# Weight fetches tied to the softmax in a fused attention and network kernel, with the first unit's normalisation on another engine

## The chip, the cores and the metric

The kernel runs on one core of a Trainium2 chip. A core has a matrix engine (TensorE, PE in the profile, with its weight loads as PEld), a vector engine (VectorE, DVE), a scalar engine (ScalarE, ACT), a general engine (GpSimd, POOL) and a queue that issues transfers (SyncE, SP). The first four work from SBUF, the on-chip memory; matmuls write to PSUM, which is handed out in banks. The metric is the device time of one execution in microseconds.

## The reference

Attention over 4 batches, 8 heads, 768 positions and 64 columns a head, in which each query sees the first four keys (the sinks) and a window of 128 keys that ends at itself; then a two-layer network on the 3072 tokens, 512 to 2048 to 512. All is float32.

```python
scores = scale * np.matmul(q, k.transpose(0, 1, 3, 2))
keep = is_sink | in_window
scores = np.where(keep, scores, -1000000000.0)
a = np.exp(scores - np.max(scores, axis=-1, keepdims=True))
a = a / (np.sum(a, axis=-1, keepdims=True) + 1e-09)
x = np.matmul(a, v)            # then heads side by side: 3072 x 512
h = x @ w_in
out = np.maximum(0.01 * h, h) @ w_out
```

The weights come as float64, that is as pairs of 32-bit words, and the kernel turns them into float32 itself.

## The kernel before

**Units.** The 3072 tokens are cut into eight units of 384 (half a batch each), and a unit has three blocks of 128 queries (T = 3). Attention runs unit by unit and head by head. The network runs one unit behind: while it works on unit u, attention works on unit u + 1. So there is a first stretch with attention alone.

**Attention, units 0 and 1 (`attend_early`).** For each block: scores on TensorE (L266), masked reduction on DVE which finds the row's maximum (L278; it becomes `anchor[0]`), exponential with row sum on ACT (L280). After three blocks `normalise_early` makes the reciprocals on DVE (L283, L284) and multiplies the probabilities: in unit 0 on DVE (L290), in unit 1 on ACT (L288). The tail transposes the probabilities on TensorE (L338, L339, L342), ACT copies them out of PSUM (L340, L343), POOL gathers the sinks' columns (L346), and `values` multiplies with the values (L407, L411). Tails and values of a head are put on a list and taken from it between the scores of the next head, so that TensorE has work while a softmax runs. In unit 0 the scores use four PSUM banks by turns, later one.

**Attention, units 2 to 7 (`attend_late`).** Here each operand is split into a rounded high part (fp32r) and the rest, and the parts are multiplied separately: `split_head` (L231 on ACT, L232 and L234 on POOL) for queries and keys, `split_values` (L245 on ACT, L246 on POOL) for the values of a pair of heads, at the even head of the pair. The tails are L351, L358 on ACT, L359 on DVE and L320 on POOL.

**Network (`mlp_stream`).** Sixteen slices `fc` of 128 hidden columns: matmuls into `h` (L525), leaky ReLU on ACT and DVE (L532, L533), split into `gh` and `gl` (L534, L535), matmuls into `o` (L546). A slice has seven steps, 112 a unit (`mlp_steps`); an attention unit has 60 (`att_steps`), and the attention's steps are dealt out between those of the network. The network starts after 70 steps of attention (60 + LEAD0).

**Weights.** There are 32 tiles of 512 KB of words, `wi` and `wo` of each slice. `load_weights(fc)` fetches both tiles of a slice on SP (L152, L153), decodes each with three DVE instructions (L169, L171, L173; the word is put together in PSUM bank `d`), rounds on ACT (L177) and subtracts on POOL (L178). A fetch waits until the decode four tiles back is done (DEPTH); the first four have no such wait. Slices 0 and 1 are asked for in the first stretch, the others by the network's first unit, two slices ahead. `check_weights` fetches all 32 tiles again in units 2 to 5, to see whether they lie in the range that the decoder handles (L187 on ACT, L189 on POOL, L191 on DVE).

**Order of work.** TensorE's instructions run in the order written. Those of the other engines are ordered when the program is built, by a planner with a model of costs and due times; each engine and SP's queue then take them strictly in that order. `tc.issue_after(anchor[0].ins)` keeps a decode behind the latest reduction on DVE. A dependency added by `tc.add_manual_dep` is a real wait on the chip.

**Banks for transpositions.** `slot()` hands them out: in the first stretch (phase 0) `t` and `h` by turns, then (phase 1) only `t`, and once every weight tile has been asked for (phase 2) `t` and the decoder's `d` by turns.

Of the kernel before, what the change touches and what calls it, by code (L numbers as in the profile page):

```python
# [9 lines left out]
F32 = mybir.dt.float32  # L10
F32R = mybir.dt.float32r
I32 = mybir.dt.int32
I8 = mybir.dt.int8
AF = mybir.ActivationFunctionType
ALU = mybir.AluOpType
# [5 lines left out]
P = 128  # L21
# [5 lines left out]
NFC = DF // P  # L27
# [27 lines left out]
PRE = 2  # L55
WARM = 22
DEPTH = 4
PRE0 = 24
PRED = 12
W_LO = 1.125 * 2.0 ** -15  # L60
W_HI = 1.875 * 2.0 ** 16
# [51 lines left out]
def fast_path(ctx, tc, cpool, qk, vu, vs, w_in, w_out, out, ident, wz, lim, masks, tri, diag, negm, wmin, wmax):  # L113
    nc = tc.nc
    wpool = ctx.enter_context(tc.tile_pool(name="wpool", bufs=1))
# [3 lines left out]
    iopool = ctx.enter_context(tc.tile_pool(name="iopool", bufs=2))  # L119
# [3 lines left out]
    ps_t = ctx.enter_context(tc.tile_pool(name="ps_t", bufs=1, space=PSUM))  # L123
# [22 lines left out]
    wts = {}  # L146
    anchor = [None]

    def fetch(raw, nm, fc):
        if nm == "i":  # L150
            src = w_in.rearrange("(c p) f -> p c f", p=P)[:, :, 2 * fc * P:2 * (fc + 1) * P]
            return nc.sync.dma_start(out=raw.rearrange("p (c f) t -> p c (f t)", c=NCC), in_=src)  # L152
        return nc.sync.dma_start(out=raw.rearrange("p f t -> p (f t)"), in_=w_out[fc * P:(fc + 1) * P, :])  # L153

    decoded = []

    def load_weights(fc):
        for nm in ("i", "o"):
            raw = wpool.tile([P, 512, 2], I32, tag=f"w{nm}{fc}", name=f"w{nm}raw{fc}")
            dma = fetch(raw, nm, fc)  # L160
            if len(decoded) >= DEPTH:
                tc.add_manual_dep(dma.ins, decoded[-DEPTH].ins.name,
                                  mybir.DependencyInfo(mybir.DependencyClass.Sync, mybir.DependencyReason.SCHED_ONLY),
                                  reason="pace")
            top, low = raw[:, :, 1], raw[:, :, 0]
            word = ps_t.tile([P, 512], I32, tag="d", name=f"d{nm}{fc}")
            w = iopool.tile([P, 512], F32, tag="io", name=f"w{nm}f{fc}")
            with tc.issue_after(anchor[0].ins):
                nc.vector.tensor_scalar(out=word, in0=top, scalar1=3, scalar2=0x3FFFFFFF,  # L169
                                        op0=ALU.logical_shift_left, op1=ALU.bitwise_and)  # L170
            nc.vector.scalar_tensor_tensor(out=word, in0=top, scalar=-0x40000000, in1=word,  # L171
                                           op0=ALU.bitwise_and, op1=ALU.bitwise_or)
            decoded.append(nc.vector.scalar_tensor_tensor(out=w.bitcast(I32), in0=low, scalar=29, in1=word,  # L173
                                                          op0=ALU.logical_shift_right, op1=ALU.bitwise_or))
            both = wpool.tile([P, 2, 512], F32R, tag=f"w{nm}{fc}", name=f"w{nm}{fc}")
            hi, lo = both[:, 0, :], both[:, 1, :]
            nc.scalar.copy(out=hi, in_=w)  # L177
            nc.gpsimd.tensor_tensor(out=lo, in0=w, in1=hi.bitcast(F32), op=ALU.subtract)  # L178
            wts[nm, fc] = (hi, lo)

    def check_weights(nm, fc):
        raw = iopool.tile([P, 512, 2], I32, tag="wraw", name=f"c{nm}raw{fc}", bufs=1)
        fetch(raw, nm, fc)
        mag = iopool.tile([P, 512], F32, tag="io", name=f"mag{nm}{fc}")
        zero = iopool.tile([P, 512], F32, tag="io", name=f"zero{nm}{fc}")
        col = (NFC if nm == "o" else 0) + fc
        nc.scalar.activation(out=mag, in_=raw.bitcast(F32)[:, :, 1], func=AF.Abs,  # L187
                             accum_out=wmax[:, col:col + 1])
        nc.gpsimd.tensor_scalar(out=zero, in0=mag, scalar1=0.0, scalar2=None, op0=ALU.is_equal)  # L189
        with tc.issue_after(anchor[0].ins):  # L190
            nc.vector.tensor_tensor_reduce(out=zero, in0=mag, in1=zero, scale=1.0, scalar=3.0e38,  # L191
                                           op0=ALU.add, op1=ALU.min, accum_out=wmin[:, col:col + 1])
# [45 lines left out]
    def split_values(u, h):  # L238
        vr, sr = vraws.pop((u, h))
        vsp = apool.tile([P, 4, 2 * P], F32R, tag="vsp", name=f"vsp{u}_{h}", bufs=1)  # L240
        ssp = apool.tile([SKR, 1, 2 * P], F32R, tag="ssp", name=f"ssp{u}_{h}", bufs=1)
        for dst, src, m in ((vsp, vr, NVB[u % 2]), (ssp, sr, 1)):
            sview = src[:, 0:m * P].rearrange("p (n q c) -> p n q c", q=2, c=D)
            hview = dst.rearrange("p n (q c) -> p n q c", c=D)[:, 0:m, 0::3, :]
            nc.scalar.copy(out=hview, in_=sview)  # L245
            nc.gpsimd.tensor_tensor(out=dst[:, 0:m, D:3 * D].rearrange("p n (q c) -> p n q c", c=D),  # L246
                                    in0=sview, in1=hview.bitcast(F32), op=ALU.subtract)
        return vsp, ssp
# [33 lines left out]
    def normalise_early(u, w, sm):  # L282
        nc.vector.tensor_scalar(out=sm, in0=sm, scalar1=1e-9, scalar2=None, op0=ALU.add)  # L283
        nc.vector.reciprocal(out=sm, in_=sm)  # L284
        for j in range(T):
            p = w[:, j, :] if u % 2 or j else w[:, j, WM:]
            if u:
                nc.scalar.mul(p, p, sm[:, j:j + 1])  # L288
            else:
                nc.vector.tensor_scalar(out=p, in0=p, scalar1=sm[:, j:j + 1], scalar2=None, op0=ALU.mult)  # L290

    def softmax(u, h, j, ps, w):
        if KSL[u % 2][j][1] == W3:
# [151 lines left out]
    def attend_late(u, h, pend, state):  # L445
        odd = h % 2
        sp = split_head(u, h)
        state = state[h // 2 % 2]
        if not odd:
            state["v"] = split_values(u, h)  # L450
            state["sk"] = apool.tile([P, T, 2, NSK], F32, tag="sk", name=f"sk{u}_{h // 2}")
        load_next(u, h)
        pk = apool.tile([P, T, WM], F32, tag="pk", name=f"pk{u}_{h}", bufs=PKB)
        sk = state["sk"]
        pt = apool.tile([P, 2, 2 * TU], F32R, tag="pt", name=f"pt{u}_{h}")
        state["pt", odd] = pt
        for j in range(T):
            ps = scores(u, h, j, (0, TU + NK[u % 2]), sp)
            softmax(u, h, j, ps, pk[:, j, :])
            yield  # L460
            at = len(pend) - (VSW and j == 0 and not odd and len(pend) > 0)
            pend.insert(at, (0, lambda j=j: tail(u, h, j, pk, pt, sk)))
# [46 lines left out]
    def mlp_stream():  # L509
        po = {}  # L510
        prev = None
        for step in range(NU * NFC + 1):
            u, fc = divmod(step, NFC)
            cur = None
            if u < NU:
                if u == 0:
                    while len(wts) < 2 * min(NFC, fc + 1 + AHEAD):
                        load_weights(len(wts) // 2)
                wh, wl = wts["i", fc]
                ph = ps_h.tile([P, 512], F32, tag="h", name=f"h{u}_{fc}")  # L520
                for cc in range(NCC):
                    xh, xl = xs[u][cc]
                    cs = slice(cc * P, (cc + 1) * P)
                    for c, (w, x) in enumerate(((wh, xh), (wh, xl), (wl, xh))):
                        nc.tensor.matmul(ph[:, 0:TU], lhsT=w[:, cs], rhs=x, start=cc == 0 and c == 0,  # L525
                                         stop=cc == NCC - 1 and c == 2)
                    if cc < NCC - 1:
                        yield
                g = mpool.tile([P, TU], F32, tag="g", name=f"g{u}_{fc}")
                gh = mpool.tile([P, TU], F32R, tag="gh", name=f"gh{u}_{fc}", bufs=2)  # L530
                gl = mpool.tile([P, TU], F32R, tag="gl", name=f"gl{u}_{fc}", bufs=2)
                nc.scalar.mul(g, ph[:, 0:TU], 0.01)  # L532
                anchor[0] = nc.vector.tensor_tensor(out=g, in0=ph[:, 0:TU], in1=g, op=ALU.max)  # L533
                nc.scalar.copy(out=gh, in_=g)  # L534
                (nc.gpsimd if u == 0 else nc.vector).tensor_tensor(out=gl, in0=g, in1=gh.bitcast(F32), op=ALU.subtract)  # L535
                cur = (u, fc, gh, gl)
                yield
# [35 lines left out]
    done = 0  # L573
    while done < att_steps + LEAD0:
        done += 1
        next(stream)
        if done >= PRE0 and len(wts) < 2 * min(PRE, (done - PRE0 + 1) // PRED):
            load_weights(len(wts) // 2)
    phase[0] = 1
    for x, _ in enumerate(mlp_stream()):  # L580
        if len(wts) == 2 * NFC:
            phase[0] = 2
        due = att_steps + LEAD0 + att_steps * (x + 1) // mlp_steps
        due += min(LEAD - LEAD0, (LEAD - LEAD0) * (x + 1) // mlp_steps)
        while done < due:
            done += 1
            next(stream, None)
# [200 lines left out]
```

## Time and profile before

| what | value |
|---|---|
| median of the runs | 740.24 us (738.78 to 741.04, 3 runs) |
| the profiled execution | 740.5 us |
| its span, first to last instruction | 738.6 us, 12473 instructions |
| PE busy | 712.1 us, 96% |
| PEld busy | 622.7 us, 84% |
| DVE busy | 547.8 us, 74% |
| ACT busy | 422.6 us, 57% |
| POOL busy | 371.2 us, 50% |
| moved by DMA | 77.77 MB, mean 105 GB/s |
| mean granted TensorE clock | 0.988 |

The profile is one execution. Each row of a timeline gives the start and duration in us, the engine, the line of the kernel (L290), the operation, output and input tiles with their shapes, how many instructions were joined (x3), and in brackets how long the engine stood before and for whom. The view of waits gives us in total, the number of times and the longest. The view of stretches gives busy time of each engine between two moments, then the granted TensorE clock (1.00 is full speed), the share of the DMA engines and GB/s. The chain of waits is followed back from the last instruction. Idle time of an engine that nobody waits for costs nothing.

### The profile page before, as it was taken

To read this page: it belongs to the slowest core of one execution; us is meant where nothing else is said; L and a number is where in the kernel's file an instruction comes from. 1 tells how busy PE (TensorE), PEld (TensorE's weight loads), DVE (VectorE), ACT (ScalarE), POOL (GpSimd) and SP (SyncE) were. 2 spreads that over 40 slices of the span, in tenths; PEclk is the share of its full clock that TensorE was granted. 3 is DMA by queue.
4 is the path that set the end of the run, shared out by engine and by line. 5 is a ranking of instruction groups with operands and counts; after the bars stand their busy time and mean duration, and the time that the engine had idled before them with its cause. 6 is when DMAs were issued, how large, how long until landed. Compare 5 with 4: busy or idle time off the path is not lost.

```text
span 738.6 us, 12473 instructions
## 1 busy us (share of the span) xinstructions
PE 712.1 (96%) x3871; PEld 622.7 (84%) x3871; DVE 547.8 (74%) x1749; ACT 422.6 (57%) x1178; POOL 371.2 (50%) x500
## 2 busy tenths in 40 slices
PE   6889999899999999999999999999999999999996
PEld 4547887689999988999988988999988999989995
DVE  6678888656667898888888988888888978733222
ACT  4566666657665566656666566666666565522221
POOL 2025556745555676756657676756566556300000
PEclk9899999999999999999999999999999999999999
DMA  8466667122112333324343343324332221001001
GB/s 295 120 208 199 211 207 231 57 87 73 50 55 69 128 108 110 115 87 157 95 126 109 114 126 123 101 100 138 115 111 94 88 69 41 0 1 43 1 1 48
DMA packets 43755, 77.77 MB, mean 105 GB/s; under 512 B 3616, under 2 KB 26400, under 8 KB 43680
## 3 DMA queue, kind: packets, MB, share of 16 engines
q1 hardware_dynamic: 43536, 76.76, 32.8%
q8 instruction: 33, 0.54, 0.3%
q14 instruction: 42, 0.34, 0.1%
q10 hardware_dynamic: 144, 0.13, 0.1%
HBM read 70.58 MB, written 6.29 MB: 104 GB/s over the span
## 4 chain that ended last, share of the span: by engine, by line
PE 82%; DVE 9%; DMA 3%; ACT 3%; issue 1%; SPq 0%; POOL 0%; ACTq 0%; DVEq 0%
PE h L525 32%; PE o L546 32%; PE v L407 8%; PE s L266 6%; PE t L351 2%; DVE gl L535 2%; DMA qkn<-in_qk 1%; DVE zeroi L191 1%; PE v L411 1%; DVE g L533 1%; DMA vsraw<-in_vs 1%; PE t L338 1%; DVE pe L278 0%; DVE xf L419 0%; DVE pk L311 0%
## 5 line engine op out<-in xcount | busy, mean ns | idle before, releaser
L525 PE MATMUL h<-xh,wi 128*128 128x384 f32 x1024 | 314.5, 354 | 1.5 <-DVE g L533 1.5
L546 PE MATMUL o<-wo,gh 128*128 128x512 f32 x768 | 244.9, 400 | 0.0
L525 PEld LDWEIGHTS h<-xh,wi 128*128 128x128 f32 x1024 | 190.5, 188 | 14.4 <-DVE g L533 2.6
L525 PE MATMUL h<-xl,wi 128*128 128x384 f32 x512 | 172.7, 337 | 0.0
L546 PE MATMUL o<-wo,gl 128*128 128x512 f32 x384 | 151.8, 395 | 0.0
L546 PEld LDWEIGHTS o<-wo,gh 128*128 128x128 f32 x768 | 134.1, 189 | 18.0 <-issue 2.4
L320 POOL TENSOR_SCALAR_AFFINE_SELECT pt<-stg 128x256 fp32r<-128x256 f32 x240 | 101.8, 450 | 83.3 <-DVE stg L359 70.0
L533 DVE TENSOR_TENSOR g<-h,g 128x384 f32<-128x384 f32 x128 | 71.0, 555 | 63.3 <-ACT g L532 61.5
L535 DVE TENSOR_TENSOR gl<-g,gh 128x384 fp32r<-128x384 f32 x112 | 93.4, 834 | 16.7 <-ACT gh L534 15.1
L532 ACT ACTIVATE g<-h 128x384 f32<-128x384 f32 x128 | 62.4, 487 | 73.0 <-PE h L525 72.8
L525 PEld LDWEIGHTS h<-xl,wi 128*128 128x128 f32 x512 | 97.1, 190 | 3.3
L232 POOL TENSOR_TENSOR qksp<-qkraw,qksp 64x392 fp32r<-64x392 f32 (+1 forms) x48 | 58.6, 1221 | 63.6 <-issue 46.7
L305 ACT ACTIVATE pk<-pk,negm 128x128 f32<-128x128 f32 (+1 forms) x144 | 58.0, 403 | 50.4 <-DVE negm L302 49.3
L546 PEld LDWEIGHTS o<-wo,gl 128*128 128x128 f32 x384 | 72.3, 188 | 16.9 <-DVE gl L535 0.3
L534 ACT CAST gh<-g 128x384 fp32r<-128x384 f32 x128 | 65.7, 513 | 32.9 <-DVE g L533 30.3
L266 PEld LDWEIGHTS s<-qksp 128*128 128x128 f32 x288 | 53.5, 189 | 6.2 <-issue 0.2
L266 PE MATMUL s<-qksp 128*128 128x260 f32 (+1 forms) x288 | 56.5, 278 | 0.0
L234 POOL TENSOR_TENSOR qksp<-qkraw,qksp 128x384 fp32r<-128x384 f32 x48 | 53.6, 1116 | 3.6
L358 ACT CAST stg<-t 128x128 fp32r<-128x128 f32 x120 | 30.8, 257 | 41.3 <-PE t L351 32.7
L407 PEld LDWEIGHTS v<-pt,vsp 128*128 128x128 f32 x336 | 45.1, 189 | 5.8 <-issue 3.3
L231 ACT CAST qksp<-qkraw 128x776 fp32r<-128x776 f32 (+1 forms) x48 | 42.8, 892 | 10.4 <-PE s L266 10.1
L311 DVE TENSOR_SCALAR pk<-pk,sm 128x132 f32<-128x132 f32 (+1 forms) x120 | 46.0, 384 | 2.4
(131 smaller groups left out, 1084.1 us busy)
## 6 DMA issues: line engine op xcount, KB each, us to landing
qkraw<-in_qk SPq DMA_DIRECT2D x27, 454.0 KB, 3.2
qkraw<-in_qk SPq DMA_DIRECT2D x26, 388.0 KB, 3.2
wiraw<-in_w_in SPq DMA_DIRECT2D x16, 512.0 KB, 3.8
woraw<-in_w_out SPq DMA_DIRECT2D x16, 512.0 KB, 4.2
ciraw<-in_w_in SPq DMA_DIRECT2D x16, 512.0 KB, 3.8
coraw<-in_w_out SPq DMA_DIRECT2D x16, 512.0 KB, 3.6
out<-ob SPq DMA_DIRECT2D x23, 256.0 KB, 2.0
vraw<-in_vu SPq DMA_DIRECT2D x14, 256.0 KB, 2.7
```

Of the source, the lines that this page charges most:

```text
L232: nc.gpsimd.tensor_tensor(out=sp[D:P, TU:TU + n], in0=raw[D:P, TU:TU + n], in1=sp[D:P, TU:TU + n].bitcast(F32), op=ALU.subtract)
L234: nc.gpsimd.tensor_tensor(out=sp[:, TU + n:2 * TU + n], in0=raw[:, 0:TU], in1=sp[:, 0:TU].bitcast(F32), op=ALU.subtract)
L266: nc.tensor.matmul(ps[:, 0:kn], lhsT=sp[:, off + j * P:off + (j + 1) * P], rhs=sp[:, TU + k0:TU + k0 + kn], start=c == 0, stop=c == len(pa ...
L305: nc.scalar.activation(out=w, in_=w, func=AF.Exp, scale=-1.0, bias=neg, accum_out=sm)
L320: nc.gpsimd.affine_select(out=out, in_=src, pattern=([[0, x]] if x > 1 else []) + [[sign, P]], base=-1 if prev else 0, channel_multiplier= ...
L407: nc.tensor.matmul(out[:, o:o + m], lhsT=l, rhs=r, start=c == 0, stop=c == len(mms) - 1, skip_group_check=True)
L525: nc.tensor.matmul(ph[:, 0:TU], lhsT=w[:, cs], rhs=x, start=cc == 0 and c == 0, stop=cc == NCC - 1 and c == 2)
L532: nc.scalar.mul(g, ph[:, 0:TU], 0.01)
L533: anchor[0] = nc.vector.tensor_tensor(out=g, in0=ph[:, 0:TU], in1=g, op=ALU.max)
L534: nc.scalar.copy(out=gh, in_=g)
L535: (nc.gpsimd if u == 0 else nc.vector).tensor_tensor(out=gl, in0=g, in1=gh.bitcast(F32), op=ALU.subtract)
L546: nc.tensor.matmul(po[t], lhsT=gg[:, tsl], rhs=w, start=f == 0 and c == 0, stop=f == NFC - 1 and c == 2)
```

## The change

Five edits are made together.

1. `load_weights` takes one tile a call instead of the two of a slice. In the first stretch it is called at the steps 20, 32, 44 and 56 (before: both tiles of a slice at 35 and at 47).
2. The first four fetches, which waited for nothing, wait for `anchor[0]`, the latest softmax reduction at that point of the program. The first fetch of `check_weights` does so too.
3. `phase` becomes 2 at the end of the network's first unit (step 112) instead of when all tiles have been asked for (the start of slice 13).
4. In units 2 to 7 the values of a pair are split at its odd head, not at its even one.
5. In unit 0 the multiplication by the reciprocal is done by POOL instead of DVE.

```diff
-PRE0 = 24
+PRE0 = 8
...
-    def load_weights(fc):
-        for nm in ("i", "o"):
-            raw = wpool.tile([P, 512, 2], I32, tag=f"w{nm}{fc}", name=f"w{nm}raw{fc}")
-            dma = fetch(raw, nm, fc)
-            if len(decoded) >= DEPTH:
-                tc.add_manual_dep(dma.ins, decoded[-DEPTH].ins.name,
...
+    def pace(dma, after):
+        tc.add_manual_dep(dma.ins, after.ins.name,
...
+    def load_weights():
+        fc, nm = len(wts) // 2, "io"[len(wts) % 2]
+        raw = wpool.tile([P, 512, 2], I32, tag=f"w{nm}{fc}", name=f"w{nm}raw{fc}")
+        dma = fetch(raw, nm, fc)
+        pace(dma, decoded[-DEPTH] if len(decoded) >= DEPTH else anchor[0])
...
     def check_weights(nm, fc):
-        fetch(raw, nm, fc)
+        dma = fetch(raw, nm, fc)
+        if fc == 0 and nm == "i":
+            pace(dma, anchor[0])
...
-                nc.vector.tensor_scalar(out=p, in0=p, scalar1=sm[:, j:j + 1], scalar2=None, op0=ALU.mult)
+                nc.gpsimd.tensor_scalar(out=p, in0=p, scalar1=sm[:, j:j + 1], scalar2=None, op0=ALU.mult)
...
-        if not odd:
-            state["v"] = split_values(u, h)
+        if odd:
+            state["v"] = split_values(u, h - 1)
+        else:
             state["sk"] = apool.tile([P, T, 2, NSK], F32, tag="sk", name=f"sk{u}_{h // 2}")
...
                     while len(wts) < 2 * min(NFC, fc + 1 + AHEAD):
-                        load_weights(len(wts) // 2)
+                        load_weights()
...
-        if done >= PRE0 and len(wts) < 2 * min(PRE, (done - PRE0 + 1) // PRED):
-            load_weights(len(wts) // 2)
+        if len(wts) < min(2 * PRE, (done - PRE0) // PRED):
+            load_weights()
...
-        if len(wts) == 2 * NFC:
+        if x >= mlp_steps:
             phase[0] = 2
```

More of the change, by code (lines that the diff above doesn't have):

```diff
@@ L155, in fast_path @@
     decoded = []
-    def load_weights(fc):
-        for nm in ("i", "o"):
-            raw = wpool.tile([P, 512, 2], I32, tag=f"w{nm}{fc}", name=f"w{nm}raw{fc}")
-            dma = fetch(raw, nm, fc)
-            if len(decoded) >= DEPTH:
-                tc.add_manual_dep(dma.ins, decoded[-DEPTH].ins.name,
[L163 to L179, printed above, removed]
@@ new lines, in pace @@
+    def pace(dma, after):
+        tc.add_manual_dep(dma.ins, after.ins.name,
+                          mybir.DependencyInfo(mybir.DependencyClass.Sync, mybir.DependencyReason.SCHED_ONLY),
+                          reason="pace")
+    def load_weights():
[3 more added lines that the diff above has]
+        pace(dma, decoded[-DEPTH] if len(decoded) >= DEPTH else anchor[0])
+        top, low = raw[:, :, 1], raw[:, :, 0]
+        word = ps_t.tile([P, 512], I32, tag="d", name=f"d{nm}{fc}")
+        w = iopool.tile([P, 512], F32, tag="io", name=f"w{nm}f{fc}")
+        with tc.issue_after(anchor[0].ins):
+            nc.vector.tensor_scalar(out=word, in0=top, scalar1=3, scalar2=0x3FFFFFFF,
+                                    op0=ALU.logical_shift_left, op1=ALU.bitwise_and)
+        nc.vector.scalar_tensor_tensor(out=word, in0=top, scalar=-0x40000000, in1=word,
+                                       op0=ALU.bitwise_and, op1=ALU.bitwise_or)
+        decoded.append(nc.vector.scalar_tensor_tensor(out=w.bitcast(I32), in0=low, scalar=29, in1=word,
+                                                      op0=ALU.logical_shift_right, op1=ALU.bitwise_or))
+        both = wpool.tile([P, 2, 512], F32R, tag=f"w{nm}{fc}", name=f"w{nm}{fc}")
+        hi, lo = both[:, 0, :], both[:, 1, :]
+        nc.scalar.copy(out=hi, in_=w)
+        nc.gpsimd.tensor_tensor(out=lo, in0=w, in1=hi.bitcast(F32), op=ALU.subtract)
+        wts[nm, fc] = (hi, lo)
```

## The prediction, made before the changed kernel was run

> **What bounds the kernel now.** I read first the busy time by stretches, cut where the work changes character: attention of the first unit alone to 56 us, then the network's first unit with the weights still arriving, then the passage to the third unit of attention, then the rest.
>
> ```profile
> 0.00:56.00 56.00, 43.98 (x191) 27.36 (x192) 35.71 (x146) 30.40 (x99) 10.95 (x29) 0.91 0.64 206
> 56.00:120.00 64.00, 63.00 (x325) 52.15 (x324) 57.02 (x123) 43.45 (x108) 37.14 (x37) 1.00 0.68 210
> 120.00:146.00 26.00, 21.70 (x108) 17.58 (x107) 18.64 (x43) 15.56 (x40) 18.19 (x18) 0.97 0.39 126
> 146.00:240.00 94.00, 94.00 (x527) 84.19 (x527) 62.22 (x223) 60.35 (x173) 48.35 (x70) 0.99 0.21 66
> 240.00:738.60 498.60, 489.45 (x2727) 441.42 (x2725) 374.24 (x1216) 272.87 (x761) 256.54 (x348) 1.00 0.27 87
> ```
>
> The second number is PE's busy time, then PEld, DVE, ACT, POOL, the granted clock, the DMA share and GB/s. From 56 to 120 us and after 146 us TensorE is full at clock 1.00: there the change can win nothing, and whatever is won earlier is carried to the end. TensorE lacks 12.0 us of work before 56 us (and the clock is 0.91) and 4.3 us from 120 to 146 us. All of the change's effect must come from these two stretches. Who is waited for there, by the view of TensorE's waits (us in total, times, longest):
>
> ```profile
> PE t L342 <- DVE pe L290: 6.2, 4, 2.1
> PE t L338 <- DVE wof L173: 3.4, 1, 3.4
> PE s L266 <- DMA qkn<-in_qk: 3.2, 1, 3.2
> ...
> PE t L338 <- ACT pt L340: 0.9, 1, 0.9
> ```
>
> Each part of the change is aimed at one of these rows, so I price them one by one against the profiled execution's own 740.5 us (span 738.6 us and 1.9 us around it). That is 0.3 us from the median of the runs, 740.24 us, so no correction is made between them.
>
> **A. The early fetches held back.** The SP queue and the chain of waits show why the fourth head's data came late:
>
> ```profile
> 6.09 0.38 SPq L152 DMA_DIRECT2D wiraw<-in_w_in  x1
> ...
> 8.10 0.92 SPq L152 DMA_DIRECT2D ciraw<-in_w_in  x1
> 9.12 2.41 SPq L201 DMA_DIRECT2D qkn<-in_qk  x2
> ```
> ```profile
> 9.12 8.77 DMA qkn<-in_qk
> ```
> ```profile
> wiraw<-in_w_in SPq DMA_DIRECT2D x16, 512.0 KB, 3.8
> ...
> qkn<-in_qk SPq DMA_DIRECT2D x6, 388.0 KB, 4.3
> ```
>
> Five fetches of 512 KB (four weight tiles and the first tile of the weight check) went out between 6.09 and 8.10 us, since nothing held them; the head's load behind them took 8.77 us where the median is 4.3. TensorE stood, and ran at a lower clock afterwards:
>
> ```profile
> 10.12 0.30 PE L342 MATMUL t<-ident,pe 128*128 128x128 f32 x1 [1.80 <-DVE pe L290]
> ...
> 17.93 0.60 PE L266 MATMUL s<-qkn 128*128 128x128 f32 x2 [3.25 <-DMA qkn<-in_qk]
> ```
> ```profile
> 10.00:20.00 10.00, 6.63 (x31) 4.43 (x32) 5.04 (x23) 4.41 (x18) 0.58 (x3) 0.91 0.86 323
> 20.00:30.00 10.00, 10.00 (x42) 6.58 (x41) 4.87 (x23) 5.11 (x19) 0.19 (x1) 0.75 0.31 94
> 140.00:152.00 12.00, 8.96 (x40) 7.46 (x41) 6.39 (x18) 6.04 (x16) 6.07 (x6) 0.86 0.11 34
> ```
>
> With the five out of the way the load lands at about 9.12 + 4.3 = 13.4 us, before TensorE asks for it at 14.68 us (17.93 less 3.25). So the wait of 3.25 us goes. The lost clock is 10 x 0.09 + 10 x 0.25 = 3.4 us of work that would not have to be made up; I take it as won too, because TensorE then has no idle time of this length there. Together 6.65 us. What is late next is the second to last head's normalisation, which belongs to C. If the clock stays low all the same, 3.4 us of it is not won.
>
> The fetches don't vanish. The new loop asks for one tile at the steps 20, 32, 44 and 56 of 70, where the old one asked for two at 35 and two at 47. Head 0 takes 3 steps, head 1 six, then 8 and 7 by turns, so the anchors are the scores' reductions of head 3, head 4, head 6 and the first head of unit 1. Behind a held fetch on SP stand the loads of the next heads (L201) and values (L214); the reduction it waits for has been issued just before, and a head's load has about two heads, 6.7 us, from issue to need (a head takes 3.33 us, rows in C), against the 3.8 and 4.3 us above. I cost this at nothing; if the cover goes, each late load costs what the 17.93 row shows. Only the first check tile is moved out of the stretch altogether; it comes back behind a reduction of the network's third unit, where the DMA share is 0.27 and the 31 other check tiles already pass.
>
> **B. Tiles decoded singly.** A decode is three DVE instructions of 0.7 us, and they get between the short steps of a softmax:
>
> ```profile
> 40.00 0.15 DVE L284 RECIPROCAL sm<-sm 128x3 f32<-128x3 f32 x1
> 40.11 0.70 DVE L171 SCALAR_TENSOR_TENSOR di<-wiraw,di 128x512 int32<-128x512 int32 x1
> 40.72 0.81 DVE L290 TENSOR_SCALAR pe<-pe,sm 128x128 f32<-128x128 f32 x3
> ```
>
> Of the 6.2 us of waits for L290, 1.80 are head 0's (row 10.12, no decode yet). The other 4.4 fall where four tiles are decoded. The four decodes remain, 4 x 3 x 0.7 = 8.4 us of DVE. Singly, one to about a head and a half, they may cost nothing (4.4 won) or delay as many steps as now (nothing won), and below that if DVE stands for a tile not landed, which is a rival below. I take the middle, 2.2 us won.
>
> **C. Normalisation on POOL.** 24 multiplications, one of 128 and two of 260 columns in each of the eight heads, go from DVE to POOL. On DVE three take 0.8 us. An undisturbed head runs so:
>
> ```profile
> 24.71 0.43 DVE L278 CUSTOM_DVE_ANT_0 pe<-s,wide 128x260 f32<-128x260 f32 x1 [0.60 <-PE s L266]
> ...
> 26.25 0.18 DVE L284 RECIPROCAL sm<-sm 128x3 f32<-128x3 f32 x1
> 26.46 0.82 DVE L290 TENSOR_SCALAR pe<-pe,sm 128x128 f32<-128x128 f32 x3
> ...
> 28.04 0.43 DVE L278 CUSTOM_DVE_ANT_0 pe<-s,wide 128x260 f32<-128x260 f32 x1 [0.38 <-PE s L266]
> ```
>
> From the last reduction of one head to that of the next: 28.04 - 24.71 = 3.33 us, and the way goes through the multiplications, since TensorE transposes blocks 0 and 1 just ahead of the scores whose reduction is the last row. So what the first two multiplications gain or lose is gained or lost per head; the third has those scores as cover. The profile has no such multiplication on POOL. The nearest rows, a one-input TENSOR_SCALAR (from the view of line 189) and a one-input select (from the page):
>
> ```profile
> L189 POOL TENSOR_SCALAR zeroi<-magi x16: 1481/1490/1702, 252.3 to 562.1; 128x512 f32<-128x512 f32 x16
> ```
> ```profile
> L320 POOL TENSOR_SCALAR_AFFINE_SELECT pt<-stg 128x256 fp32r<-128x256 f32 x240 | 101.8, 450 | 83.3 <-DVE stg L359 70.0
> ```
>
> By the first, 2.9 ns a column: 0.37 + 0.76 = 1.13 us for the first two, against 0.5 on DVE, 0.63 us more per head. By the second, 1.76 ns a column: 0.68 us, 0.18 more. DVE gets 8 x 0.8 = 6.5 us free, but I count no gain from that beyond B's: TensorE is full from 20 to 30 us (10.00 of 10 above), so a shorter way over DVE would only make DVE wait. I take the first row, the same kind of instruction: 8 x 0.63 = 5.0 us lost, with 0 and 5.0 as bounds and a dearer case below. Behind the multiplications on POOL stand the decodes' remainders (L178, 1.28 us, a row below), which are not due before the network starts; where a remainder stands ahead of them instead, a head loses up to 1.28 us, four times at most, which the middle value of B has to cover. [...]
>
> **D. Late values.** The split of the values moves from an even head to the odd one after it. At its first use ACT stood for the small transfer, with TensorE's copies behind it:
>
> ```profile
> 125.99 0.30 ACT L245 CAST ssp<-vsraw 128x128 fp32r<-128x128 f32 x1 [1.98 <-DMA vsraw<-in_vs]
> ```
>
> A head later the data is there; the 0.9 us wait of the table above goes. The values' matmuls come only after the odd head, so nobody asks for the split sooner. Its POOL part is queued behind one more head's split: no cost while TensorE is covered, 0.9 us if it isn't.
>
> **E. The decode bank.** Transpositions borrow the decoder's PSUM bank once phase is 2. Now this happens when the last tiles have been asked for, so TensorE waits for the last decode (L173): the 3.4 us row. The new test waits for the end of the network's first unit, 112 steps, when the last decode is long due. The wait goes, and of the low clock after it 12 x 0.14 = 1.7 us. In exchange the transpositions of some 24 steps share one bank, and a bank is free only after ACT's copy:
>
> ```profile
> L358 ACT CAST stg<-t 128x128 fp32r<-128x128 f32 x120 | 30.8, 257 | 41.3 <-PE t L351 32.7
> ```
>
> With a subtraction of about the same length that is half a us where two follow each other; I allow 0.8 us, bounds 0 and 2. Net 3.4 + 1.7 - 0.8 = 4.3 us.
>
> **Sum:** 6.65 + 2.2 - 5.0 + 0.9 + 4.3 = 9.05 us won; 740.5 - 9.0 = 731.5 us. A measurement of this kernel can tell about 0.3%, 2.2 us, from no change.
>
> **The rivals.** (1) POOL is cheap: C is nothing, 726.5 us. For it the select row, against it the L189 row. Chance 0.24. (2) POOL and DVE get in each other's way. A DVE instruction on three columns (median 170 ns by the view of its line) took 0.82 us while POOL ran:
>
> ```profile
> L283 DVE TENSOR_SCALAR sm<-sm x16: 147/170/816, 9.3 to 131.0; 128x3 f32<-128x3 f32 x16
> ```
> ```profile
> 44.15 0.82 DVE L283 TENSOR_SCALAR sm<-sm 128x3 f32<-128x3 f32 x1
> ```
> ```profile
> 43.67 1.28 POOL L178 TENSOR_TENSOR wi<-wif,wi 128x512 fp32r<-128x512 f32 x1 [1.81 <-DMA woraw<-in_w_out]
> ```
>
> It ended with POOL's. If POOL's multiplications hold every head's L283 like that, 8 x 0.65 = 5.2 us more: 736.7 us. Against it: by the cycle above POOL would be done just about when L283 comes. Chance 0.12. [...] (3) DVE stands for the tiles. It takes instructions in the order written; if the planner puts a decode right behind the reduction that releases the fetch, DVE stands up to 3.8 us (landing row) for each of four tiles, with all softmax work behind it: 15.2 us, 746.7 us, slower. It decides from 9.05 / 4 = 2.3 us per tile. For it: the fetches of now go out at 6 to 8 us, the decode row above is at 40 us, and the new fetches have no such lead. Against it: the decode may be placed after other heads' work. Chance 0.10. (4) The gains are waited off: the earlier start meets weights no sooner ready, and the bank wait changes into one for a single bank; D alone stays, 739.6 us, no change. For it DVE at 57.0 of 64 us; against it TensorE, not DVE, is full there. Chance 0.09.
>
> **The numbers.** The forecast has 0.45: with B and E at their ends, 728.5 (B 4.4, one bank free) to 735 (B nothing, the bank 2 us). Faster are it and rivals 1 and 2: 0.81; the same, rival 4: 0.09; slower, rival 3: 0.10. The range holds the 0.81: from 723.5 (rival 1 with B at 4.4 and no bank cost) to 738 (rival 2 with B at nearly nothing).
>
> **What would show it.** A: no wait of scores for qkn near 15 us, clock near 1 from 10 to 30 us, first fetches after 14 us. B: no decode between L284 and the multiplication, shorter waits. C: duration of L290 on POOL, near 0.76 us for 260 columns, and a head's cycle near 4 us; 3.3 would be rival 1. Long L283 beside POOL is rival 2; DVE idle until wiraw or woraw is rival 3. D and E: no waits at L245 and L173 at 110 to 145 us; the network's first matmul some 4 us sooner than now, at about 52 us (6.65 + 2.2 - 5.0 = 3.85). Wrong in whole if that first matmul is not earlier, or if its lead is gone at 120 us.

## The result and the profile after

| | before | after |
|---|---|---|
| median | 739.51 us (736.39 to 741.04, 4 runs) | 750.31 us (746.72 to 751.99, 4 runs) |
| the profiled execution | 740.5 us, clock 0.988 | 746.72 us, clock 0.987 |
| its span | 738.6 us | 745.0 us |

The change makes the kernel slower: the ratio is 1.0156, with an interval from 1.0117 to 1.0194. The forecast was 731.5 us, with a range from 723.5 to 738. The runs after lie further apart than those before, and the clock goes with them: 746.72 us at 0.987, 751.99 us at 0.979. The profiled execution is the fastest of the four. Ratios here and below are of fast runs against fast runs of the kernel before in the same series; one run of e5 (1158.8 us) and one of e12 (2454.32 us) are left out of them. The change itself was run in the first series only.

First the busy time by stretches of the kernel after, cut at the same moments as before (PE, PEld, DVE, ACT, POOL, clock, DMA share, GB/s):

```profile
0.00:56.00 56.00, 43.86 (x168) 25.52 (x168) 24.13 (x107) 25.37 (x83) 28.73 (x51) 0.85 0.55 173
56.00:120.00 64.00, 58.94 (x295) 46.78 (x296) 53.13 (x118) 41.41 (x106) 32.08 (x32) 1.00 0.63 196
120.00:146.00 26.00, 25.52 (x132) 20.95 (x131) 21.78 (x49) 18.93 (x48) 19.12 (x20) 1.00 0.66 211
146.00:240.00 94.00, 92.85 (x525) 82.96 (x525) 62.59 (x221) 60.56 (x173) 50.21 (x69) 1.00 0.19 61
```

From 120 to 146 us TensorE is now nearly full at clock 1.00, as the forecast said (E). The loss is nearly all ahead of that (1.15 us of TensorE's time lie idle between 146 and 240 us). In the first 56 us TensorE is busy about as long as before (43.86 against 43.98 us), but with 168 records instead of 191, at a clock of 0.85 instead of 0.91: it gets less done. The network's first matmul starts at 63.93 us, before at 55.74 us, and forecast was 52.

```profile
63.93 0.44 PE L530 MATMUL h<-xh,wi 128*128 128x384 f32 x1
```

Who TensorE waits for, after (in total, times, longest):

```profile
PE t L346 <- POOL pe L294: 4.9, 2, 3.0
PE h L530 <- DVE g L538: 2.7, 2, 2.5
PE s L270 <- DVE negm L282: 2.0, 1, 2.0
PE t L342 <- POOL pe L294: 1.8, 3, 0.6
```

The waits of 3.2 us for `qkn` and of 3.4 us for the last decode (`wof`) are gone, as forecast. In their place stands POOL's multiplication, and once the reduction (`negm`). Is POOL too slow? One step further back, the timeline of DVE says otherwise:

```profile
20.81 0.43 DVE L282 CUSTOM_DVE_ANT_0 pe<-s,wide 128x260 f32<-128x260 f32 x1 [1.78 <-PE s L270]
...
21.71 0.43 DVE L282 CUSTOM_DVE_ANT_0 pe<-s,wide 128x260 f32<-128x260 f32 x1
...
25.05 0.69 DVE L171 TENSOR_SCALAR di<-wiraw 128x512 int32<-128x512 int32 x1 [2.90 <-DMA wiraw<-in_w_in]
25.65 0.16 DVE L287 TENSOR_SCALAR sm<-sm 128x3 f32<-128x3 f32 x1
...
26.52 0.17 DVE L288 RECIPROCAL sm<-sm 128x3 f32<-128x3 f32 x1
...
45.60 0.69 DVE L171 TENSOR_SCALAR di<-wiraw 128x512 int32<-128x512 int32 x1 [1.67 <-DMA wiraw<-in_w_in]
...
56.36 0.69 DVE L171 TENSOR_SCALAR do<-woraw 128x512 int32<-128x512 int32 x1 [2.20 <-DMA woraw<-in_w_out]
```

On POOL and on TensorE the same moment reads:

```profile
26.89 2.43 POOL L294 TENSOR_SCALAR pe<-pe,sm 128x128 f32<-128x128 f32 x3 [4.98 <-DVE sm L288]
```
```profile
27.55 0.33 PE L346 MATMUL t<-ident,pe 128*128 128x128 f32 x1 [2.95 <-POOL pe L294]
28.46 0.33 PE L342 MATMUL t<-ident,pe 128*128 128x128 f32 x1 [0.58 <-POOL pe L294]
```

The view of waits names POOL, but POOL itself stood 4.98 us for the reciprocal on DVE, and DVE stood 2.90 us for a weight tile, with the sum (L287) and the reciprocal (L288) of head 3 queued behind the decode. The tile had been fetched only at 21.32 us, since its fetch is now held by that same head's last reduction but one (row 20.81, done by 21.25 us). The last one (row 21.71) still runs, and then the decode stands. The issues on SP and the chain of waits:

```profile
21.32 0.38 SPq L152 DMA_DIRECT2D wiraw<-in_w_in  x1
...
41.17 0.38 SPq L152 DMA_DIRECT2D wiraw<-in_w_in  x1
...
52.12 0.33 SPq L153 DMA_DIRECT2D woraw<-in_w_out  x1
```
```profile
21.32 3.69 DMA wiraw<-in_w_in
...
41.17 4.33 DMA wiraw<-in_w_in
...
52.12 4.22 DMA woraw<-in_w_out
```

Each of the three lands about 4 us after its issue, and DVE stands for it 2.90 + 1.67 + 2.20 = 6.8 us in all. Before there was no such wait. What comes on top is the clock, by stretches of the kernel after:

```profile
10.00:20.00 10.00, 8.75 (x35) 5.32 (x35) 2.92 (x15) 4.55 (x17) 5.82 (x10) 0.83 0.27 87
20.00:30.00 10.00, 6.28 (x27) 3.48 (x26) 4.14 (x15) 4.70 (x15) 4.96 (x7) 0.94 0.50 157
30.00:40.00 10.00, 9.48 (x31) 5.86 (x29) 4.82 (x19) 4.43 (x16) 3.30 (x6) 0.55 0.53 175
40.00:50.00 10.00, 6.71 (x31) 3.98 (x31) 4.38 (x14) 4.45 (x14) 7.28 (x9) 0.96 0.62 197
50.00:60.00 10.00, 7.90 (x30) 4.03 (x29) 4.58 (x20) 4.69 (x15) 3.32 (x7) 0.87 0.59 193
```

Lost clock is 10 us times what is missing to 1.00: 1.7 + 0.6 + 4.5 + 0.4 + 1.3 = 8.5 us up to 60 us. From 30 to 40 us TensorE looks busy, 9.48 of 10, and does about half the work: six matmuls of the values (L411, 128 x 256) take 2.40 us from 31.53 us on, at clock 0.50, and 1.30 us from 44.52 us on, at 1.00. This is the stretch behind the stand at 27.55 us.

### The profile page after: what moved, and what is told of

The parts are those of the page before. It is cut to its first block, busy times and chain, and to the rows that moved or that the text cites. A ratio compares the mean times of both kernels' runs of the same rounds, so it can differ in the third digit from the quotient of the medians.

```text
span 745.0 us, 12487 instructions
## 1 busy us (share of the span) xinstructions
PE 716.1 (96%) x3871; PEld 622.5 (84%) x3871; DVE 540.0 (72%) x1725; ACT 423.6 (57%) x1178; POOL 390.6 (52%) x524
## 4 chain that ended last, share of the span: by engine, by line
PE 81%; DVE 8%; ACT 3%; DMA 2%; issue 2%; POOL 2%; SPq 0%; POOLq 0%; ACTq 0%; DVEq 0%
PE o L551 32%; PE h L530 32%; PE v L411 8%; PE s L270 6%; PE t L355 2%; DVE gl L540 1%; DMA wiraw<-in_w_in 1%; POOL pe L294 1%; ACT pe L284 1%; DVE zeroi L195 1%; DVE g L538 1%; PE v L415 1%; DVE pe L282 1%; DMA woraw<-in_w_out 1%; DMA vsraw<-in_vs 1%
## 5 line engine op out<-in xcount | busy, mean ns | idle before, releaser
L411 PEld LDWEIGHTS v<-pt,vsp 128*128 128x128 f32 x336 | 45.0, 189 | 5.6 <-issue 3.1
```

What stands on the lines that cost most here:

```text
L411: nc.tensor.matmul(out[:, o:o + m], lhsT=l, rhs=r, start=c == 0, stop=c == len(mms) - 1, skip_group_check=True)
```

## The experiments

**Theory.** The held fetch leaves a tile some 4 us on its way, and the planner, which orders DVE when the program is built, puts the decode ahead of the same head's sum. While DVE does the multiplications itself, other work comes first; once POOL does them, DVE's list is shorter and the decode comes close behind the reduction that releases its fetch. So the hold and POOL together cost what neither does alone. In this form I hold the theory only since the first four runs. Their expectations still keep the two causes apart (theory 1, DVE stands for held tiles; theory 2, POOL's multiplications), and two of the four were missed: e1 came out 6.5 us below the lowest time expected of it, e2 9.5 us. **Rivals.** POOL's multiplications are the whole loss; or the held fetches are, whatever engine multiplies; or the later edits (bank, values) go wrong.

The first four kernels take the parts apart.

**e1_free**: the change with its first four fetches not held (the weight check's first fetch still is).

```diff
-        pace(dma, decoded[-DEPTH] if len(decoded) >= DEPTH else anchor[0])
+        if len(decoded) >= DEPTH:
+            pace(dma, decoded[-DEPTH])
```

> The changed kernel, but the first four weight fetches wait for no reduction any more (the check's first fetch is still held, decodes stay single, POOL normalises). Theory 1 (DVE stands for held tiles: 2.9, 1.7 and 2.2 us before its decodes in the changed kernel's profile, with clock lost after each stand): those three waits are gone, 6.8 us and some 2 us of clock won, 3 to 6 us given back because the fourth head's data is late again: 744 to 748 us. Theory 2 (the POOL multiplications, 2.43 us a head instead of 0.8, are the loss): no better than 749 us.

Measured: 737.53 us against 737.7 before, ratio 0.9997 (0.9983 to 1.0010).

**e2_dve**: the change with the multiplications back on DVE, fetches held.

```diff
-                nc.gpsimd.tensor_scalar(out=p, in0=p, ...
+                nc.vector.tensor_scalar(out=p, in0=p, ...
```

> The changed kernel, with unit 0's multiplications on DVE as before; fetches still held. Theory 2 (POOL): the first two multiplications of a head take 0.5 us again instead of 1.5, 8 heads, so 8 us won: about 742 us. Theory 1 (held fetches): DVE still stands for three or four tiles and the POOL time lay beside those stands: 747 us or more.

Measured: 732.53 us, ratio 0.9925 (0.9906 to 0.9945).

**e3_free_dve**: both of these edits.

> The changed kernel with both undone: fetches not held and multiplications on DVE; left are single decodes at steps 20, 32, 44 and 56, the held check fetch, late values and the later use of the decode bank. If theories 1 and 2 together are the whole loss: faster than before by the bank's share, 734 to 737 us. If the single, earlier decodes cost by themselves: 740 us or more.

Measured: 735.34 us, ratio 0.9961 (0.9945 to 0.9976).

**e4_bank_late**: the kernel before with only the late values and the bank's test (`if x >= mlp_steps`).

> The kernel before with only two edits: values split at the odd head, and the decode bank lent to transpositions only after the network's first unit. As forecast (0.9 + 4.3 us): 734.5 us, without the 3.4 us wait for the last decode. Rival, the wait changes hands (in the changed kernel a transposition waits 1.15 us for the single bank and a score 1.3 us for a reduction): 737 to 739 us.

Measured: 733.96 us, ratio 0.9942 (0.9925 to 0.9959).

What follows: with the hold and POOL 1.0156, with either alone 0.9925 and 0.9997, with neither 0.9961. On DVE the hold is a gain of 0.4%, on POOL a loss of 1.6%. That is an interaction, so neither of the first two rivals can be the whole; and e4 rules out the third. The order of DVE's instructions shows how the two meet (kernel after on the left, e2 on the right, from the last reduction of head 3 on; reductions that lie between are left out where they don't matter):

```
after                          e2_dve
L282 reduction, head 3         L282 reduction, head 3
L171 decode of wi   <- stands  L282 reduction, head 4
L287 sum, head 3               L287 sum, head 3
L282 reduction, head 4         L288 reciprocal, head 3
L173 decode                    L294 multiplications x3
L288 reciprocal, head 3        L282 reduction, head 4
                               L171 decode of wi
```

In e2 the same tile is fetched at 19.45 us, and this is DVE's timeline:

```profile
20.94 0.17 DVE L287 TENSOR_SCALAR sm<-sm 128x3 f32<-128x3 f32 x1 [0.39 <-ACT pe L284]
21.14 0.18 DVE L288 RECIPROCAL sm<-sm 128x3 f32<-128x3 f32 x1
21.36 0.82 DVE L294 TENSOR_SCALAR pe<-pe,sm 128x128 f32<-128x128 f32 x3
...
23.14 0.69 DVE L171 TENSOR_SCALAR di<-wiraw 128x512 int32<-128x512 int32 x1 [0.63 <-DMA wiraw<-in_w_in]
```

DVE finishes the head first, and by then the tile is nearly there: 0.63 us of standing instead of 2.90.

That was read from orders and traces. The next four kernels move the decode alone, and try the two partners on the kernel before.

**e5_lead**: the change, hold and POOL included; `load_weights` is cut in two, and each of the first four tiles is decoded 8 attention steps after its fetch.

```diff
...
-        if len(wts) < min(2 * PRE, (done - PRE0) // PRED):
-            load_weights()
+        if len(fetched) < min(2 * PRE, (done - PRE0) // PRED):
+            fetch_weights()
+        if len(wts) < min(2 * PRE, (done - PRE0 - 8) // PRED):
+            decode_weights()
```

> The changed kernel (held fetches, POOL multiplications), but each of the first four tiles is decoded eight attention steps after its fetch is asked for, so that on DVE the head's sum, reciprocal and the next reductions stand between. Theory 1 (DVE stands, in front of a head's sum, for a tile that is still on its way, and TensorE's clock falls in the stands): DVE's waits for wiraw and woraw, 6.8 us in the changed kernel, fall below 1 us and the time to 733 to 738 us. Theory 2 (POOL's 2.4 us a head are enough by themselves once TensorE isn't held up by data): 744 us or more.

Measured: 736.03 us against 737.42 before, ratio 0.9976 (0.9960 to 0.9993).

**e6_lead_dve**: the same with the multiplications on DVE.

> The same lead, with the multiplications on DVE. Theory 1: the 1.4 us that DVE still stood with held fetches and DVE multiplications go, 1 to 2 us better than that kernel's 732.5: 730.5 to 732. If later decodes only crowd the start of the network: 733 to 735.

Measured: 733.97 us, ratio 0.9953 (0.9933 to 0.9974).

**e7_pool_only**: the kernel before with the multiplications on POOL.

> The kernel before with one edit: unit 0's multiplications on POOL. Nothing is held, tiles decoded in pairs. By POOL's measured prices (0.6 and 0.93 us) the first two multiplications of a head are 1.0 us later, 8 us for eight heads if all of it is on TensorE's path. Theory 1: part of it is hidden, since with unheld fetches POOL cost 2.2 us beside the single decodes: 739 to 742 us against 737.7. Theory 2: 744 us or more.

Measured: 741.56 us, ratio 1.0059 (1.0035 to 1.0082).

**e8_hold_only**: the kernel before, its first four fetches and the weight check's first held by `anchor[0]`, tiles in pairs.

> The kernel before with one edit: the first four fetches and the check's first one wait for the latest reduction (pairs asked for at steps 35 and 47, multiplications on DVE). The fourth head's wait of 3.25 us and the low clock after it should be gone. As forecast (6.65 us won): 731 us. If DVE stands for the tiles here too, two at a time: 736 us or more.

Measured: 734.78 us, ratio 0.9965 (0.9947 to 0.9983).

What follows: moving nothing but the decodes takes 1.8% off the changed kernel. Up to the first decode DVE takes its instructions in the same order in e5 and in the change; from there on e5's head 3 is finished first. With DVE multiplying, the same lead gains nothing (e6 0.9953, e2 0.9925), since there DVE hardly stood. On the kernel before, POOL alone costs 0.6% (e7) and the hold alone gains 0.35% (e8): nothing like the 1.6%. e5's trace has no wait of DVE for these tiles (the first decode now starts at 26.05 us, 3.66 us after its fetch at 22.39), the network starts at 54.90 us, and the clock is lost once, not three times:

```profile
10.00:20.00 10.00, 7.54 (x31) 4.63 (x32) 3.17 (x17) 4.87 (x20) 5.24 (x8) 0.83 0.32 101
20.00:30.00 10.00, 9.40 (x45) 5.40 (x43) 5.40 (x22) 6.04 (x22) 5.50 (x9) 1.00 0.61 197
30.00:40.00 10.00, 8.67 (x40) 4.70 (x38) 5.77 (x21) 6.58 (x22) 8.65 (x12) 1.00 0.76 248
40.00:50.00 10.00, 7.30 (x34) 3.82 (x32) 6.12 (x21) 5.45 (x19) 5.17 (x8) 1.00 0.83 291
50.00:60.00 10.00, 8.14 (x38) 5.07 (x36) 8.00 (x22) 7.66 (x23) 2.94 (x4) 1.00 0.59 181
```

The two traces account for each other. From 10 to 60 us TensorE's busy time is 41.05 us in e5 and 39.12 after, 1.9 us less (2.9 less from the start on). The lost clock is 1.7 us in e5 and 8.5 after, 6.8 more. Together 9.7 us; the network starts 63.93 - 54.90 = 9.0 us later and the span is 745.0 - 734.9 = 10.1 us longer. In these two executions over two thirds of the loss is clock, which no row of a wait shows.

The last four kernels price the other parts and put the good ones together.

**e9_best**: e8 with the late values and the bank's test as in the change; pairs, DVE.

> The kernel before with the held fetches, the late values and the bank's test; the tiles stay in pairs and the multiplications on DVE. If the ratios of the single parts multiply (held 0.9965, bank and values 0.9942): 0.9907, about 730.7 us of 737.5, the fastest so far. If what the held fetches win before 60 us is waited off when the weights are late for the network (the forecast's fourth rival), no better than bank and values alone: 0.994, 733.1 us. If single decodes were worth the 2.2 us that the forecast gave them, this kernel is as much above the held kernel with DVE's multiplications (0.9925) as that: 0.995 or more.

Measured: 731.49 us against 737.76 before, ratio 0.9899 (0.9879 to 0.9919).

**e10_bank_only**: the kernel before with the bank's test alone.

```diff
-        if len(wts) == 2 * NFC:
+        if x >= mlp_steps:
```

> The kernel before with the bank's test alone. The forecast gave this 4.3 us (3.4 of wait and 1.7 of clock won, 0.8 lost to the single bank): 0.9942. The theory after the second batch: the wait goes and the lost clock too, but two short waits for the single bank and a longer one at the network's start come in: 2.5 to 4 us, 0.9946 to 0.9966. If the bank were the whole of what bank and values win together (0.9942), the values are worth nothing.

Measured: 734.36 us, ratio 0.9943 (0.9924 to 0.9962).

**e11_late_only**: the kernel before with the late values alone.

```diff
-        if not odd:
-            state["v"] = split_values(u, h)
+        if odd:
+            state["v"] = split_values(u, h - 1)
+        else:
```

> The kernel before with the late values alone. The forecast gave it 0.9 us: 0.9988. The theory from the trace of the changed kernel: ACT's split stays where it was in the order and still stands for the small transfer, TensorE waits 0.5 us instead of 0.9: at most 0.5 us, a ratio of 0.9993 to 1.000, not to be told from none. If the values' POOL part, a head later, met the decodes' remainders, slower by up to 0.9 us.

Measured: 737.94 us, ratio 0.9998 (0.9985 to 1.0011).

**e12_first_lead**: e5, but only the first tile has the 8 steps; the other three are decoded at their fetch.

```diff
-        if len(wts) < min(2 * PRE, (done - PRE0 - 8) // PRED):
+        if len(wts) < min(2 * PRE, (done - PRE0 - (0 if wts else 8)) // PRED):
```

> The changed kernel with only the first of the four tiles decoded 8 steps after its fetch; the other three are decoded right at their fetch, as in the change. The changed kernel stands to the one before as 1.0156, with a lead for all four as 0.9976, so 1.8% or 13.3 us lie between. If a wait of DVE costs by its own length, the first tile has 2.9 of 6.8 us: 43% of it goes, 1.008. If what counts is that TensorE stands long enough to lose clock, the first tile (two waits of 3.0 and 0.6 us on TensorE and the clock of 0.55 from 30 to 40 us behind it) is most of it: 7 to 10 us, 1.002 to 1.006. If the wait just moves to the next tile, nothing is gained: 1.0156.

Measured: 744.64 us, ratio 1.0070 (1.0046 to 1.0094).

What follows: e9 is the fastest kernel of the study, 1.0% below the one before; it is near the product of its parts, so the fourth rival of the forecast (gains waited off) is out. e10 takes the whole of what e4 won, and e11 nothing that can be measured. For e10 I had expected less; its ratio lies at the forecast's 0.9942. In e12 DVE stands 3.2 us for tiles instead of 6.8, and about half of the loss against e5 is left: 1.0070 - 0.9976 = 0.9% of 1.8%. So the loss goes roughly with the length of DVE's waits, about two us for each; that the first tile is most of it is not borne out, though the interval of e12 touches that expectation's upper end. How one wait becomes two is to be seen in e12. DVE stands 2.85 us for a tile until 51.66 us, and so does TensorE; the rows are of e12's DVE, of its TensorE and of its stretches:

```profile
51.66 0.69 DVE L178 TENSOR_SCALAR do<-woraw 128x512 int32<-128x512 int32 x1 [2.85 <-DMA woraw<-in_w_out]
```
```profile
52.74 1.23 PE L277 MATMUL s<-qkn 128*128 128x260 f32 x2 [2.35 <-DVE negm L289]
```
```profile
50.00:60.00 10.00, 6.83 (x18) 3.30 (x18) 4.14 (x13) 3.77 (x12) 0.98 (x2) 0.58 0.42 128
60.00:70.00 10.00, 8.90 (x35) 6.62 (x35) 6.16 (x16) 6.08 (x19) 2.00 (x5) 0.73 0.37 125
```

The clock falls at about 51.7 us (0.85 from 51 to 52 us, 0.50 from 52 to 53), inside this one stand of 2.35 us, and from there 4.2 + 2.7 = 6.9 us of clock are lost.

## Why the prediction was wrong, point by point

**The step that failed** is the end of A: "The fetches don't vanish … I cost this at nothing." It asked what a held fetch delays on SP's queue, and found cover there: the heads' loads behind the fetches. It didn't ask who is waiting at the other end. The consumer of a held tile is a DVE instruction, DVE takes its list strictly in order (in the kernel after, ACT has the last row sum of head 3 ready at 22.79 us, and the sum on it starts at 25.65 us, behind the decode), and a fetch that is released by a reduction can be missed by what stands a few places on in that list: in each of the three waits one more reduction and one other short instruction lay between. The third rival said this in words (a decode right behind the reduction that releases its fetch, DVE standing, softmax work behind it), with a chance of 0.10 and a time of 746.7 us. The mechanism was that one; that its 746.7 us lie near the measured 750.31 is luck, as the sizes in it show. Three sizes in it were off. The wait was 6.8 us in all for four tiles, 1.7 a tile, not 3.8. It decided already there, below the 2.3 us a tile that I gave as the point, because each us cost two through the clock (13.3 us between e5 and the change), a factor that the rival didn't have. And the 9.05 us that it was set against weren't there to be won.

**What the argument against the rival missed** is that C makes it likely. "The decode may be placed after other heads' work" holds with DVE multiplying (e2: 0.63 and 0.8 us of waits) and not with POOL. I counted DVE's 6.5 us set free as neither gain nor loss. An engine whose order is planned with a cost model is rearranged by work that leaves it; that the freed time is what draws the decode forward is inferred from the two orders, since the planner's own costs weren't looked at. Where C and the hold meet without a lead, C's price is 1.0156 / 0.9925, some 2.3%.

**A, 6.65 us forecast; 2.6 us measured alone (e8), 3.2 us beside bank and values (e9 against e4).** The mechanism was right: no wait for `qkn`, and in e8 the network starts at 48.93 us, 6.8 us sooner than in the trace of before. Of that, e8's span keeps 5.1 us (738.6 to 733.5): the wait for the last decode is there in both (3.4 us), but the clock from 120 to 146 us is 0.87, before 0.97. The other part is the trace of before itself. Its 3.4 us of clock were one execution's: behind the same wait e10, whose code is the same up to there, shows a clock of 0.58 from 20 to 30 us and e11 one of 0.92.

```profile
20.00:30.00 10.00, 10.00 (x34) 6.33 (x32) 3.24 (x14) 3.91 (x15) 0.19 (x1) 0.58 0.22 66
```
```profile
20.00:30.00 10.00, 10.00 (x48) 6.30 (x47) 5.23 (x25) 5.69 (x22) 0.38 (x2) 0.92 0.36 111
```

From 10 to 20 us all three show 0.91, so the lost clock of this stand is 0.9 + 4.2 = 5.1 us in e10, 1.7 in e11 and 3.4 in the trace of before. The forecast took a term that changes that much from run to run at the value of one run, and that run, at 740.5 us, was 3 us above the medians of 737.4 to 737.8 us that before showed later.

**B, 2.2 us won forecast; none.** Kernels with single tiles lie above their twins with pairs: e2 0.9925 against e9 0.9899, e3 0.9961 against e4 0.9942, 1.4 to 1.9 us. The intervals overlap in both cases, e2 and e9 weren't run in one series, and e3 holds the check's first fetch where e4 doesn't, so a small loss is likely rather than shown. A gain of 2.2 us doesn't fit them: from the far ends of the intervals it would be about 1 us at most (0.9906 against 0.9919, 0.9945 against 0.9959). My middle value was a guess between two ends, and what lies below the lower end I had put into a rival.

**C, 5.0 us lost forecast; 4.4 us in e7.** The total is near, but by two errors that cancel. From the view of the line, after:

```profile
L294 POOL TENSOR_SCALAR pe<-pe,sm x24: 604/934/937, 9.8 to 53.9; 128x260 f32<-128x260 f32 x16, 128x128 f32<-128x128 f32 x8
```

A multiplication of 260 columns takes 0.93 us and one of 128 columns 0.60, so by a straight line through the two the slope is 0.33 us for 132 columns, 2.5 ns a column, and the rest, an estimated 0.28 us, is fixed. For 512 columns that gives 1.56 us; the L189 row has 1.49. I had 0.76 and 0.37 us: a row of 512 columns hides the fixed part. The first two multiplications take 1.53 us, 1.03 more than the 0.5 us on DVE, in eight heads 8.2 us. And I had taken all of it to lie on the path, while nearly half or more is hidden (4.4 us of it are seen in e7, 2.7 in e1 against e3, 1.7 in e5 against e6). Three multiplications take 2.43 us on POOL (row 26.89 above) and 0.82 us on DVE (row 21.36 of e2). Rival 1 (POOL cheap) is out by these rows, and by the sign that the forecast named: in e5 the last reductions of heads 3 and 4 start at 22.77 and 27.07 us, a cycle of 4.30 us where 3.33 would have been the rival. That the move costs nothing, which is this rival's term and C's bound of 0, no run shows; e7 shows 4.4 us in its place. Rival 2 (POOL's multiplications hold every head's sum) is out as well: the median of the sums at L287 is still 0.17 us, and the few long ones come after 76 us, in unit 1, where POOL does no multiplications.

```profile
L287 DVE TENSOR_SCALAR sm<-sm x16: 149/169/817, 9.2 to 140.2; 128x3 f32<-128x3 f32 x16
```

**D, 0.9 us forecast; nothing (e11 0.9998).** The split didn't move on the chip. It is written a head later, but the planner issues it where it did: in all three traces ACT has it between the rounding of a `wo` tile and an exponential, and ACT still stands for the small transfer with TensorE's copies behind it. ACT in e11 and after:

```profile
123.04 0.30 ACT L245 CAST ssp<-vsraw 128x128 fp32r<-128x128 f32 x1 [1.80 <-DMA vsraw<-in_vs]
```
```profile
135.15 0.30 ACT L249 CAST ssp<-vsraw 128x128 fp32r<-128x128 f32 x1 [1.52 <-DMA vsraw<-in_vs]
```

Before it was 1.98 us. Here too I read the order from the code and not from the engine's list.

**E, 4.3 us forecast; 4.2 us measured (e10).** Right, with its mechanism: no wait for L173, clock 1.00 from 130 to 150 us in e10, and one new wait of 1.1 us for the single bank (`PE t L351 <- DVE pt L359`), where I had allowed 0.8.

**The sum.** With the measured sizes it would have been 2.7 (A without the check's fetch, e2 against e3) - 1.6 (B, the middle of 1.4 and 1.9) - 2.7 (C beside single tiles) + 0 (D) + 4.2 (E) = 2.6 us won, and e5, which has all five parts and a lead for the tiles, wins 1.8 us (0.9976; 0.5 to 2.9 by its interval). The 13.3 us from there to the change are the tiles that DVE stood for, and what the clock made of it.

## What to carry to other kernels

A fetch held back until some event needs its consumer at least one landing time (here 3.7 to 4.3 us) behind that event on the consumer's own engine: look up what stands next on that list, not only what is queued behind the fetch. Where a planner orders the engines, an edit that takes work off one engine can change the order of what is left, so two edits that are harmless alone should be tried together and apart. And where TensorE ends up waiting too, price the clock with it: here DVE's stands cost about twice their length in all (13.3 us for 6.8). For a single wait of TensorE no such factor holds: one of 2.35 us went with 6.9 us of lost clock (e12), one of 2.04 us (before, until 36.68 us) with none.

## What the runs showed of the hardware

The clock comes back in steps. In the trace of before it is 0.50 from about 18.2 to 25.0 us and for 3.4 us near 50 us; after for 10.2 us from 28.7 us on; in e5 once for 3.4 us; in e12 for 13.6 us from 51.7 us on: whole multiples of 3.4 us. The lost clock before 60 us is accordingly 1.7 us or a multiple of it: 1.7 in e1, e5, e8 and e11, 3.4 in e2, e4, e6 and e9, 5.1 in e3 and in the kernel before, 6.8 in e7 and e10, 8.5 after; in e12, whose last spell runs past 60 us, it is 12.0 before 70 us. The falls and rises of one trace also lie whole multiples of about 3.4 us apart (before: 18.2, 25.0, 48.9 and 52.3 us). Stretches of e5, of after and of before, one each:

```profile
13.00:16.80 3.80, 3.77 (x13) 2.24 (x13) 1.08 (x6) 1.34 (x6) 2.00 (x5) 0.58 0.34 105
```
```profile
28.50:38.90 10.40, 9.88 (x29) 6.24 (x30) 4.00 (x15) 4.26 (x16) 4.80 (x7) 0.51 0.53 170
```
```profile
18.20:25.00 6.80, 6.80 (x20) 4.20 (x20) 1.50 (x6) 2.12 (x7) 0.00 (x0) 0.50 0.19 62
```

The last row shows why this is easily overlooked: TensorE is busy in all of the 6.80 us. What decides whether a stand is followed by a fall these runs do not show. Ahead of the falls at 18.2 us (before) and at 28.7 us (after) lie stands of 3.25 and 2.95 us, and in e12 the fall comes 1.3 us into a stand of 2.35 us; stands of 1.80 and 2.04 us (before, until 10.12 and 36.68 us) and of 1.97 and 2.50 us (after, until 57.45 and 70.88 us) were followed by none. The length alone, then, does not decide it: 2.35 us with a fall stand against 2.50 us without. Why TensorE stays at half for 3.4 us in one case and for 10.2 or 13.6 us in another, though it is busy, is open, as is why e10 and e11, whose code is the same up to there, differ behind the same wait.
